# Loading batch 3's K and Q right behind batch 2's V, with its crossbar transposes placed three slots sooner

## Chip, cores and metric

One core of one Trainium2 chip. The metric is the device time of one execution in microseconds (us).

An execution's time is about 1.7 us longer than the span of its profile (315.07 against 313.4, for instance). Times are compared with times, and spans with spans.

## The reference

Attention over a sliding causal window of 64 tokens, then a low-rank token mixer and a channel MLP. B = 8 batches, H = 8 heads, S = 576 tokens, D = 64, model width 512, hidden width 2048.

```python
scores = q @ k.T / sqrt(D); masked to 0 <= i - j < 64; attn = softmax(scores); x = attn @ v
h  = x.transpose(0, 2, 1) @ U @ V          # over tokens, rank 32
u  = x + h.transpose(0, 2, 1)
out = u + relu(u @ w_ch1) @ w_ch2
```

## The kernel before

The MLP runs over 9 chunks of 512 tokens. Between its groups of matmuls ("slots") the attention of the next batch is woven in. K and Q of the batches from 2 on are loaded by POOL's software DMA queue as float32, cast to bfloat16 on the way, and transposed by SP's DMA transposes (the crossbar). The parts that matter here, with cuts marked:

```python
def load_kq(b, split):              # b >= 2: 5 tiles of K and of Q, ten DMAs on POOL's queue
    ...
    nc.gpsimd.dma_start(out=dst[0:rows, t, :, :],
                        in_=src[b, :, t * P : t * P + rows, :].rearrange("h p d -> p h d"))

def load_v(b): ...                  # five DMAs of 128 KB on POOL's queue (4 into vA, 1 into vB)

def TX(t):                          # tile t: K, then Q, from SP
    def f():
        for dst, src in ((kx, kb), (qx, qb)):
            nc.sync.dma_start_transpose(
                out=dst[:, t, :, :], in_=src[:, t, :, :].rearrange("p h d -> p (h d)"))
    return f
...
CROSS = {                           # chunk: {batch: slots of its five TX}
    0: {2: [16, 17, 18, 19, 20]},
    1: {3: [13, 14, 15, 16, 17], 4: [26, 27, 28, 29, 30]},
    2: {5: [24, 25, 26, 27, 28]},
}
...
def loads(b, *tiles):
    for t in tiles:                 # the "hold": POOL copies one element of a transposed tile,
        nc.gpsimd.tensor_copy(      # so what follows on POOL waits until that transpose landed
            out=held[:], in_=qfs[(b + 1) % 2][0:1, t * HP * P : t * HP * P + 1])
        if t == tiles[0] and len(tiles) > 1:
            load_v(b + 1)
    for _ in load_kq(b + 2, False):
        pass

if 1 < b and b + 1 < B:
    load_v(b + 1)
...
if b == 1:
    slots[20].append(lambda: loads(1, 2, NT - 1))   # hold tile 2, V(2), hold tile 4, K/Q(3)
if b == 2:
    slots[15].append(lambda: loads(2, 2))           # hold tile 2 of batch 3, then K/Q(4)
```

So POOL does, from 60 us on: hold on batch 2's third transpose pair, V(2), hold on batch 2's last transpose, K/Q(3), V(3), hold on batch 3's third transpose pair, K/Q(4). "V(2)" means the V loads of batch 2.

The softmax here doesn't subtract the row's maximum and nothing guards it: scores larger than these inputs give would overflow.

Of the kernel before, what the change touches and what calls it, by code (L numbers as in the profile page):

```python
# [16 lines left out]
def kernel(  # L17
# [63 lines left out]
    NT = 5  # L81
# [28 lines left out]
    def load_kq(b, split):  # L110
        kb, qb = staged(b)
        if b < NGR:
            for h0, h1 in ((0, 4), (4, 8)) if split else ((0, H),):
                hs = slice(h0, h1)
                for t, src in ((kb, k), (qb, q)):
                    nc.gpsimd.dma_start(  # L116
                        out=t[:, hs, :, :].rearrange("p h c d -> p h (c d)"),
                        in_=src[b, hs, :, :].rearrange("h (p c) d -> p h (c d)", c=GR),
                    )
                    yield  # L120
        else:
            for t in range(NT):
                rows = P if t < NFULL else W
                for dst, src in ((kb, k), (qb, q)):
                    nc.gpsimd.dma_start(  # L125
                        out=dst[0:rows, t, :, :],
                        in_=src[b, :, t * P : t * P + rows, :].rearrange("h p d -> p h d"),
                    )
                yield

    def load_v(b):
        for t in range(NFULL + 1):
            dst, lo = (vA[b % 2][:, t], t * P) if t < NFULL else (vB[b % 2][:, NFULL - 1], S - P)
            nc.gpsimd.dma_start(  # L134
                out=dst[:, :, 0:D], in_=v[b, :, lo : lo + P, :].rearrange("h p d -> p h d")
            )

    def shift_v(b, copy):
        va, vb = vA[b % 2], vB[b % 2]
        n = NFULL - 1  # L140
        copy(out=vb[W:P, 0:n, :, :], in_=va[W:P, 0:n, :, :])
        copy(out=vb[0:W, 0:n, :, :], in_=va[0:W, 1 : n + 1, :, :])

    def shift_high(b, copy, t):
        copy(out=vB[b % 2][W:P, t, :, :], in_=vA[b % 2][W:P, t, :, :])

    def shift_low(b, copy, t):
        copy(out=vB[b % 2][0:W, t, :, :], in_=vA[b % 2][0:W, t + 1, :, :])
# [501 lines left out]
    def mlp(c):  # L650
# [93 lines left out]
    PLACE_3 = {**PLACE, "SV": [5, 5, 6, 6]}  # L744
    CROSS = {
        0: {2: [16, 17, 18, 19, 20]},
        1: {3: [13, 14, 15, 16, 17], 4: [26, 27, 28, 29, 30]},
        2: {5: [24, 25, 26, 27, 28]},
    }
    CROSS_N = [20, 21, 22, 23, 24]  # L750
# [77 lines left out]
    for c in range(NCH):  # L828
        slots = all_slots[c]

        def place(b, parts, where):
            if b not in att:
                att[b] = attention(b)
            for part in parts:
                for f, s in zip(att[b][part], where[part]):
                    all_slots[c + s // 100][s % 100].append(f)

        b = c + 1
        if b < B:
            if b == 1:  # L840
                for _ in load_kq(2, False):
                    pass

            def loads(b, *tiles):
                for t in tiles:
                    nc.gpsimd.tensor_copy(  # L846
                        out=held[:],
                        in_=qfs[(b + 1) % 2][0:1, t * HP * P : t * HP * P + 1],
                    )
                    if t == tiles[0] and len(tiles) > 1:  # L850
                        load_v(b + 1)
                for _ in load_kq(b + 2, False):
                    pass

            if 1 < b and b + 1 < B:
                load_v(b + 1)
            if 2 < b and b + 2 < B:
                loads(b, 2)
            where = {1: PLACE_1, 2: PLACE_2, 3: PLACE_3}.get(b, PLACE)
            if b < NXB:  # L860
                place(b, ("T",), where)
            if b == 1:
                place(0, ("V",), PLACE_0)
                slots[6].append(lambda: nc.scalar.copy(out=ub[1][:], in_=uf[1][:]))
            if 3 < b + 1 < B:
                slots[24].append(lambda bs=b + 1: shift_v(bs, nc.vector.tensor_copy))
            if b <= 3:

                def land(t, b=b):
                    def f():  # L870
                        if t < NFULL - 1:
                            shift_high(b, nc.scalar.copy, t)
                        if t > 0:
                            shift_low(b, nc.vector.tensor_copy, t - 1)
                    return f

                att[b]["SV"] = [land(t) for t in range(NFULL)]
                place(b, ("SV",), where)
            place(b, ("S", "M", "PV"), where)
            for n, at in CROSS.get(c, {c + 3: CROSS_N}).items():  # L880
                if n < B:
                    place(n, ("T",), {"T": at})
            place(b, ("U", "V", "UT"), where)
            if b == 1:
                slots[20].append(lambda: loads(1, 2, NT - 1))
            if b == 2:
                slots[15].append(lambda: loads(2, 2))
        for fill, extra in zip(mlp(c) + [lambda: None], slots):
            fill()
            for f in extra:  # L890
                f()
# [30 lines left out]
```

## Time and profile before

| | before |
|---|---|
| median of 3 runs | 313.64 us (313.63 to 318.27) |
| the profiled run | 315.07 us, span 313.4 us |
| PE busy | 306.1 us, 98% |
| PE's wait for batch 3's last transpose | 1.0 us |

The page of the kernel before: engines' busy time and share of the span, then the DMA queues with packets, MB and packet time as a share of the time of 16 engines, then the busy share of the DMA engines in 40 equal slices of the span, in tenths (9 is 90% or more).

```profile
span 313.4 us, 6904 instructions
PE 306.1 (98%) x2875; PEld 150.9 (48%) x2875; DVE 162.2 (52%) x298; ACT 108.6 (35%) x174; POOL 101.3 (32%) x133
q0 software_dynamic: 104720, 18.88, 82.5%
q1 hardware_dynamic: 51744, 20.55, 39.2%
DMA  7999999999999999999999999965100520020012
```

PE is the limit. The DMA engines are busy as well: 90% or more in slices 2 to 26, that is up to about 204 us. (The queues' shares add up packet times that can overlap. They pass 100% in some stretches, so they say nothing of how near a queue is to its limit.) The waits of PE between 50 and 135 us (in total, times, longest), and the chain of waits of the kernel before in that place (start, duration, what):

```profile
PE low L340 <- DMA qf<-qr: 1.0, 1, 1.0
```

```profile
89.14 0.38 SPq L299
...
89.60 5.37 DMA qf<-qr
94.98 0.14 issue
95.11 0.19 PE low L340
```

This is the wait that the change is after. Batch 3's last transpose is issued at 89.60 and lands at 94.98; PE has stood since about 94.0. Behind it stands what POOL and SP do. POOL's timeline of the kernel before (start, duration, engine, line, what; the bracket is idle time and its releaser):

```profile
60.79 0.18 POOL L846 COPY held<-qf 1x1 bf16<-1x1 bf16 x1 [9.38 <-DMA qf<-qr]
61.29 3.53 POOL L134 DMA_DIRECT2D vA<-in_v_dram  x4 [0.32 <-issue]
64.78 0.91 POOL L134 DMA_DIRECT2D vB<-in_v_dram  x1
68.55 0.18 POOL L846 COPY held<-qf 1x1 bf16<-1x1 bf16 x1 [2.85 <-DMA qf<-qr]
69.06 0.89 POOL L125 DMA_DIRECT2D kr<-in_k_dram  x1 [0.34 <-PE psA L663]
...
76.68 0.76 POOL L125 DMA_DIRECT2D qr<-in_q_dram  x1
77.36 3.60 POOL L134 DMA_DIRECT2D vA<-in_v_dram  x4
```

SP's timeline of the kernel before: the first, the seventh and the tenth of batch 3's transposes (SPq is SP's instruction queue).

```profile
74.62 1.20 SPq L299 DMA_TRANSPOSE kf<-kr  x1
...
83.39 3.16 SPq L299 DMA_TRANSPOSE kf<-kr  x1
...
89.60 1.37 SPq L299 DMA_TRANSPOSE qf<-qr  x1
```

### The profile page before, as it was taken

The page shows a single profiled execution, that of the slowest core. Times are in us where ns is not written, and L with a number is a line of the kernel's source. Part 1 is how long each engine was busy: PE and PEld are TensorE (multiplying, and loading weights), DVE is VectorE, ACT ScalarE, POOL GpSimd, SP SyncE. Part 2 cuts the span into 40 slices and gives each one's busy share as a digit, 9 for nine tenths or more (in the row PEclk, how much of TensorE's full clock was granted, in tenths as well). Part 3 has the DMA queues.
Part 4 walks back from the last instruction along what each step waited for, and adds up shares of the span by engine and source line. Part 5 has one row for each costly group of instructions (what it writes and reads, how often), then busy time and mean ns, then how long its engine had stood idle before and what let it go on. Part 6 is the DMA issues. An engine that isn't in the chain of part 4 may idle for free.

```text
span 313.4 us, 6904 instructions
## 1 busy us (share of the span) xinstructions
PE 306.1 (98%) x2875; PEld 150.9 (48%) x2875; DVE 162.2 (52%) x298; ACT 108.6 (35%) x174; POOL 101.3 (32%) x133
## 2 busy tenths in 40 slices
PE   8899999999998999999999999999999999999996
PEld 7554554544444544454445444544454444444443
DVE  4475468337756843684358445744574443016011
ACT  3655660467027520533043404440345003301500
POOL 8683263159439346426543571000000000000000
PEclk9999999999999999999999999999999999999999
DMA  7999999999999999999999999965100520020012
GB/s 104 164 208 208 206 168 146 129 180 192 121 153 200 159 152 147 193 140 159 175 174 156 170 156 158 178 99 131 67 2 2 134 84 2 14 86 33 2 61 73
DMA packets 156495, 39.87 MB, mean 127 GB/s; under 512 B 145040, under 2 KB 151440, under 8 KB 156464
## 3 DMA queue, kind: packets, MB, share of 16 engines
q0 software_dynamic: 104720, 18.88, 82.5%
q1 hardware_dynamic: 51744, 20.55, 39.2%
q8 instruction: 22, 0.36, 0.4%
q14 instruction: 9, 0.07, 0.1%
HBM read 37.97 MB, written 9.44 MB: 151 GB/s over the span
## 4 chain that ended last, share of the span: by engine, by line
PE 81%; DMA 13%; POOL 3%; DVE 2%; issue 1%; SPq 0%; POOLq 0%
PE psU L687 36%; PE psA L663 36%; DMA qr<-in_q_dram 4%; DMA vB<-in_v_dram 4%; DMA vA<-in_v_dram 3%; PE psv L581 2%; PE xw L402 2%; PE sc L340 2%; DMA qf<-qr 2%; DVE xs L469 1%; POOL vA L134 1%; PE pshh L501 1%; POOL kr L116 1%; PE tpu L613 0%; POOL vrep L220 0%
## 5 line engine op out<-in xcount | busy, mean ns | idle before, releaser
L687 PE MATMUL psU<-w2b,c 128*128 128x512 bf16 (+2 forms) x592 | 131.3, 373 | 0.1
L663 PE MATMUL psA<-uTc,w1b 128*128 128x512 bf16 x576 | 131.0, 379 | 0.0
L687 PEld LDWEIGHTS <-c 128*128 128x128 bf16 x592 | 56.6, 98 | 64.8 <-issue 0.5
L663 PEld LDWEIGHTS <-w1b 128*128 128x128 bf16 x576 | 54.2, 98 | 64.4 <-issue 1.8
L675 ACT ACTIVATE c<-psA 128x512 bf16<-128x512 f32 x84 | 50.1, 597 | 88.8 <-PE psA L663 88.2
L697 DVE TENSOR_TENSOR osb<-psU,un 128x512 f32<-128x512 f32 (+2 forms) x37 | 24.9, 677 | 76.7 <-PE psU L687 76.3
L673 DVE TENSOR_SCALAR c<-psA 128x512 bf16<-128x512 f32 x60 | 41.3, 689 | 25.5 <-PE psA L663 25.5
L594 DVE TENSOR_TENSOR un<-psv,xs 128x512 bf16<-128x512 f32 (+1 forms) x40 | 25.5, 685 | 22.9 <-PE psv L581 22.7
L134 POOL DMA_DIRECT2D vA<-in_v_dram x32 | 28.6, 909 | 17.3 <-PE psU L687 3.1
L360 ACT ACTIVATE pts<-sc 128x1024 bf16<-128x1024 f32 x32 | 31.3, 1028 | 2.7 <-PE sc L340 2.7
L125 POOL DMA_DIRECT2D kr<-in_k_dram x30 | 25.8, 860 | 10.1 <-DMA vA<-in_v_dram 3.5
L125 POOL DMA_DIRECT2D qr<-in_q_dram x30 | 25.9, 864 | 8.9 <-DMA w2b<-in_moe_w_ch_dram 3.2
L393 ACT ACTIVATE ptl<-low 128x256 bf16<-128x256 f32 x6 | 2.3, 384 | 64.4 <-PE high L340 64.4
L366 DVE TENSOR_TENSOR pts<-pts,maskA 128x1024 bf16<-128x1024 bf16 x28 | 19.1, 682 | 1.1 <-ACT pts L360 1.1
L469 DVE TENSOR_TENSOR xs<-xw,rcw 128x896 bf16<-128x896 f32 x14 | 15.3, 1092 | 0.5
L340 PEld LDWEIGHTS <-kf 64*64 64x64 bf16 x704 | 9.9, 107 | 8.8 <-issue 8.2
L846 POOL COPY held<-qf 1x1 bf16<-1x1 bf16 x6 | 1.1, 178 | 39.4 <-DMA qf<-qr 39.4
L581 PE MATMUL psv<-hh,vrep 128*128 128x512 bf16 x40 | 12.5, 379 | 0.0
L402 PEld LDWEIGHTS <-pts 128*64 128x64 bf16 x512 | 10.0, 110 | 4.7 <-issue 3.7
L340 PE MATMUL sc<-qf,kf 64*64 64x128 bf16 (+1 forms) x608 | 11.6, 212 | 0.6 <-DVE qf L293 0.6
L134 POOL DMA_DIRECT2D vB<-in_v_dram x8 | 7.2, 901 | 5.9 <-DMA qr<-in_q_dram 2.5
L616 ACT COPY uTc<-tpu 128x512 bf16<-128x512 bf16 x9 | 5.3, 586 | 10.8 <-PE tpu L613 10.8
(108 smaller groups left out, 171.2 us busy)
## 6 DMA issues: line engine op xcount, KB each, us to landing
out_dram<-osb SPq DMA_DIRECT2D x35, 256.0 KB, 5.0
vA<-in_v_dram POOLq DMA_DIRECT2D x32, 128.0 KB, 13.1
kr<-in_k_dram POOLq DMA_DIRECT2D x24, 128.0 KB, 8.7
qr<-in_q_dram POOLq DMA_DIRECT2D x24, 128.0 KB, 8.9
w2b<-in_moe_w_ch_dram POOLq DMA_DIRECT2D x4, 512.0 KB, 15.7
vB<-in_v_dram POOLq DMA_DIRECT2D x8, 128.0 KB, 13.7
w1b<-in_moe_w_ch_dram POOLq DMA_DIRECT2D x2, 512.0 KB, 10.9
w1b<-in_moe_w_ch_dram POOLq DMA_DIRECT2D x1, 1024.0 KB, 10.0
```

The costliest lines, as they stand in the source:

```text
L125: nc.gpsimd.dma_start(out=dst[0:rows, t, :, :], in_=src[b, :, t * P : t * P + rows, :].rearrange("h p d -> p h d"),)
L134: nc.gpsimd.dma_start(out=dst[:, :, 0:D], in_=v[b, :, lo : lo + P, :].rearrange("h p d -> p h d"))
L340: nc.tensor.matmul(sc[g][r0 : r0 + W, col * W : (col + n) * W], keys_of(j, u, rs), queries_of(j, blk, n, rs), start=not spare, stop=last o ...
L360: nc.scalar.activation(out=dst, in_=sc[:], func=ACT.Exp, scale=scale)
L366: nc.vector.tensor_tensor(out=dst, in0=dst, in1=maskA.rearrange("p g n w -> p g (n w)"), op=ALU.mult)
L581: nc.tensor.matmul(ps[0][:, n, :], vrep[:, off : off + P], hh["sb"][:], start=True, stop=True)
L594: nc.vector.tensor_tensor(out=u_tiles[g][rs, :], in0=ps[0][rs, n, :], in1=x[rs, t, :, :].rearrange("p h d -> p (h d)"), op=ALU.add,)
L663: nc.tensor.matmul(ps[i][:], w1b[:, dc, i * P : (i + 1) * P], uTc[:, :, dc, :], start=(dc == 0), stop=(dc == NDC - 1),)
L673: nc.vector.tensor_relu(out=c1[i][:], in_=ps[i][:])
L675: nc.scalar.activation(out=c1[i][:], in_=ps[i][:], func=ACT.Relu)
L687: nc.tensor.matmul(acc[t][:, lo:hi], c1[i][:, t * P : (t + 1) * P], w2b[:, i, lo:hi], start=(i == 0), stop=(i == NFC - 1),)
L697: nc.vector.tensor_tensor(out=osb[:, lo:hi], in0=acc[t][:, lo:hi], in1=u_tiles[g][:, lo:hi], op=ALU.add,)
```

## The change

The intent: the second hold keeps POOL idle until 68.55 us. Without it, K/Q(3) goes out right behind V(2), batch 3's transposes can start sooner, and PE need not wait at 95 us.

```diff
-        1: {3: [13, 14, 15, 16, 17], 4: [26, 27, 28, 29, 30]},
+        1: {3: [10, 11, 12, 13, 14], 4: [26, 27, 28, 29, 30]},
...
-                    if t == tiles[0] and len(tiles) > 1:
-                        load_v(b + 1)
+                if b == 1:
+                    load_v(b + 1)
                 for _ in load_kq(b + 2, False):
                     pass
...
-                slots[20].append(lambda: loads(1, 2, NT - 1))
+                slots[20].append(lambda: loads(1, 2))
```

## The prediction

> **What bounds the kernel now.** The page gives PE 306.1 us busy of a 313.4 us span, at granted clock 1.0. The waits by engine give PE 3.7 us in all; the only one the change can touch is 1.0 us on "low" (line 340) for DMA qf<-qr. In the chain of waits it ends at 94.98 us: batch 3's last crossbar transpose was issued at 89.60 and landed 5.4 us later. The table of stretches agrees: 94 to 96 us has PE busy 1.00 of 2.00. After 95 us PE never waits for a load, so the ceiling of the gain is about 1.0 us, 0.3%.
>
> **What the change does.** The instruction order of PE, DVE, ACT and SP is the same before and after. So "three slots sooner" moves nothing on SP: the ten transposes follow the same four output stores and start when K's first tile lands. The real edit is one POOL copy less ("held", 0.18 us), whose wait for batch 2's last transpose ended at 68.55. Without it POOL issues batch 3's K/Q from about 65.7 (V's fifth issue: 64.78 plus 0.91) instead of 69.06: 3.4 us sooner.
>
> **How much arrives.** Little of that. Batch 2's V loads, issued 61.3 to 65.7, landed at 66.1, 67.8, 70.0, 71.0 and 73.3, slowed by transposes and four 256 KB stores; K's first tile landed at 74.5. Both are on the software queue, and the Trainium skill (DMA: Bandwidth & Descriptors, "Two DMAs through the same engine are not ordered") says descriptors of one queue on one engine start in order. So K queues behind V: estimate, V's last landing 73.3 plus one tile at the observed pace (0.87 us) = 74.1, 0.4 us sooner. The packets dip for roughly 0.7 us between V's last and K's first, an upper estimate. The transposes follow at SP's pace (74.62 to 89.60, mostly 1.2 to 1.5 us each, one of 3.16 in a DMA stall near 83 us), so their end moves by the same 0.4 to 0.7. Batch 3's V loads come sooner too, so the contention moves along. PE's wait at 95 us should shrink from 1.0 to 0.3-0.6 us.
>
> **Cost.** Batch 2's transposes landed just before 68.5 and PE needs them at 68.81: almost no slack. K/Q descriptors queued from about 67.5 us may slow them where an engine has finished its share of V: 0 to 0.5 us of new PE wait. That also makes PE later at 95, so the two don't add fully.
>
> **Predicted.** 313.2 us, range 312.4 to 314.4. One of three runs before took 318.27, which the range leaves out.
>
> **What would show it.** POOL's timeline: K/Q issues from near 65.7, one held fewer, and a wait at about the eighth issue (eight loads outstanding). First batch 3 transpose on SP between 73.8 and 74.4, not 71. PE's wait at 95 us under 0.7 us, later work shifted by that alone. If the first transpose starts near 71.5, queueing behind V was wrong and the whole 1.0 us is gained. If PE waits on "low" near 69 us, the removed hold had protected batch 2's transposes.
>
> **What would make it wrong.** The stall near 83 us (packets over 1 us long) costs batch 3's transposes about 2 us and is tied to nothing I can see: without it the wait at 95 would be zero already; a longer one costs more. Batch 2's transposes delayed by over 1 us would make the change slightly slower. Nothing comes near 2%.

## The result

Ratios are the mean time of one kernel's runs over that of the other's of the same rounds, so not quite the ratio of the medians. Executions over 1.5% slower than the fastest of the same kernel are left out of the means.

| | before | after |
|---|---|---|
| median | 313.70 us (6 runs, 313.23 to 318.27) | 314.61 us (6 runs, 314.06 to 315.48) |
| ratio to before | 1 | 1.0029 (95%: 1.0007 to 1.0052) |
| span of the profiled run | 313.4 us | 313.4 us |

The time is within 2% of before, as forecast, but on the wrong side: 0.3% longer instead of 0.15% shorter, and 0.2 us above the range. The profiled run of before was one of its long ones, so the two traces have the same span: the difference of the medians can't be read from these two traces alone.

The changed kernel's waits of PE, which answer to the one wait of before:

```profile
PE low L340 <- DMA qf<-qr: 1.0, 1, 1.0
PE xw L402 <- DVE vB L148: 0.3, 1, 0.3
PE psU L687 <- issue: 0.2, 1, 0.2
```

The wait at 95 us has not shrunk, and a second one stands at 104 us. (The third has no releaser that the profile shows.) POOL's timeline after the change:

```profile
60.43 0.18 POOL L846 COPY held<-qf 1x1 bf16<-1x1 bf16 x1 [9.51 <-DMA qf<-qr]
60.94 3.52 POOL L134 DMA_DIRECT2D vA<-in_v_dram  x4 [0.32 <-PE psA L663]
64.41 0.91 POOL L134 DMA_DIRECT2D vB<-in_v_dram  x1
65.28 0.93 POOL L125 DMA_DIRECT2D kr<-in_k_dram  x1
...
70.68 0.88 POOL L125 DMA_DIRECT2D qr<-in_q_dram  x1 [0.97 <-PE psA L663]
...
74.61 0.69 POOL L125 DMA_DIRECT2D qr<-in_q_dram  x1
76.43 3.51 POOL L134 DMA_DIRECT2D vA<-in_v_dram  x4 [1.14 <-DVE vB L148]
```

The hold is gone. K/Q(3) starts at 65.28 instead of 69.06, but its ten issues now have gaps (with eight loads outstanding POOL waits for V(2), whose last three tiles landed at 70.15, 71.07 and 72.53). They end at 74.61, 2 us sooner than before, and V(3) starts 0.9 us sooner. SP's timeline and the chain of waits after the change:

```profile
73.38 1.83 SPq L299 DMA_TRANSPOSE kf<-kr  x1
...
88.98 1.97 SPq L299 DMA_TRANSPOSE qf<-qr  x1
```

```profile
88.98 5.75 DMA qf<-qr
94.73 0.14 issue
94.86 0.19 PE low L340
...
103.45 0.59 DVE vB L148
...
104.08 0.39 PE xw L402 x13
```

The wait at 104 us is not one for a load: V(3) had landed by 93.79. DVE worked without a pause from 99.93 us on, and PE waited for its copy into vB.

The first transpose went out 1.24 us sooner, and the last one landed only 0.25 us sooner. Since this run's V(2) also started 0.35 us sooner (60.94 against 61.29), the last landing is, counted from there, not sooner at all: 33.8 us after V(2)'s first issue against 33.7. Below, this count "from V(2)'s first issue" is used for all traces, because it takes out how fast PE and the weights' loads got through the first 60 us. The landings come from the trace's times from issue to landing.

### The profile page after: what moved, and what is told of

Same layout as the page of the kernel before. It is cut to its first block, busy times and chain, and to the rows that moved or that the text cites. A ratio compares the mean times of both kernels' runs of the same rounds, so it can differ in the third digit from the quotient of the medians.

```text
span 313.4 us, 6881 instructions
## 1 busy us (share of the span) xinstructions
PE 304.5 (97%) x2852; PEld 151.0 (48%) x2875; DVE 162.5 (52%) x298; ACT 108.6 (35%) x174; POOL 100.8 (32%) x132
## 4 chain that ended last, share of the span: by engine, by line
PE 92%; DVE 4%; DMA 2%; ACT 1%; issue 1%; SPq 0%
PE psA L663 39%; PE psU L687 37%; PE sc L340 3%; PE psv L581 3%; PE xw L402 2%; DMA qf<-qr 2%; PE unread L757 2%; PE tpg L276 1%; DVE xs L469 1%; PE pshh L501 1%; ACT pts L360 1%; DVE c L673 1%; PE xr L402 1%; PE tpm L276 0%; DVE qf L293 0%
## 5 line engine op out<-in xcount | busy, mean ns | idle before, releaser
L687 PE MATMUL psU<-w2b,c 128*128 128x512 bf16 (+2 forms) x573 | 130.0, 374 | 1.2 <-issue 0.2
```

The lines of the kernel that those rows point to most:

```text
L687: nc.tensor.matmul(acc[t][:, lo:hi], c1[i][:, t * P : (t + 1) * P], w2b[:, i, lo:hi], start=(i == 0), stop=(i == NFC - 1),)
```

## The experiments

All kernels here compute the right result. Each came with six runs (e5: five) and one trace. "Baseline" is the kernel before as run between the others in the same rounds. After "Measured" stand the ratio to the baseline, its 95% interval and the median.

### e1 and e2: controls

e1 is the kernel before, unchanged. e2 is the slots alone:

```diff
-        1: {3: [13, 14, 15, 16, 17], 4: [26, 27, 28, 29, 30]},
+        1: {3: [10, 11, 12, 13, 14], 4: [26, 27, 28, 29, 30]},
```

> The kernel before, unchanged, as a control (A/A) and to see a second profile of it. Theory P (typical run of before has no wait at 95 us): the profiled run of before took 315.07 us with span 313.4, while its other runs have a median of 313.7, about 1.4 us less; so this kernel's typical span should be near 312.0, and its profile should show the PE wait on low for DMA qf<-qr at 95 us as under 0.3 us instead of 1.0. Rival N (noise only): ratio to before 1.000 within 0.001, but the wait at 95 us stays about 1.0 us also in this profile.

> Only the slots of batch 3's transposes moved (10 to 14), the hold kept. The instruction order of every engine is that of before, waits too. Theory: the same time as before, ratio 1.000 within 0.0015. Rival: if the slots matter by something that the instruction order does not show, the ratio is that of the whole change, 1.003.

Measured: e1 0.9991 (0.9969 to 1.0013), 314.02 us, PE's wait at 95 us 0.5 us. e2 1.0002 (0.9980 to 1.0025), 314.61 us, no wait at 95 us. Theory P was half right: e1's trace has a shorter wait, but not under 0.3 us, and its span is 312.7 us, not 312.0. The slots do nothing, which the unchanged instruction order of SP said. The same program has the wait with 1.0, 0.5 or 0 us: it is not a fixed cost. In e2 PE came later (it had waited 1.0 us for Q loads in the first 50 us), and by then the transposes were there.

### e3 and e4: the hold alone, and the whole change again

e3 takes the change without the slots; e4 is the change.

> Only the second hold removed, the slots of batch 3's transposes left at 13 to 17. Theory: all of the change's effect is here, ratio 1.002 to 1.004 to before, equal to the whole change within 0.001, and POOL's K/Q issues from about 65.5 us. Rival (slots carry it): ratio 1.000.

> The whole change once more, on the same chip as the three others. Theory: ratio 1.002 to 1.004 (0.6 to 1.2 us), PE wait at 95 us of about 1 us in its profile as before, and a wait of about 0.3 us on DVE's copy into vB at 104 us. Rival N (chip to chip noise): ratio within 0.001 of 1.000.

Measured: e3 1.0027 (0.9996 to 1.0057), 315.41 us; e4 1.0020 (0.9995 to 1.0046), 314.85 us. Both in the expected range, neither interval clear of 1. e3's trace has no wait at 95 us (PE was late), e4's has 1.0 us; neither had 0.3 us at 104 us, so that expectation failed.

### e5 and e6: the place in the row, and the missing instruction

e5 is the change as the first of its row. e6 is the change, with the second hold put back on tile 2, which the first hold has waited for already, so that it holds nothing. Against the kernel before, with the slots and the line that keeps V(2) between the two copies cut:

```diff
...
-                slots[20].append(lambda: loads(1, 2, NT - 1))
+                slots[20].append(lambda: loads(1, 2, 2))
```

> The whole change a third time, now first in the row of kernels instead of last, to rule out that its place in the row made it slow. Theory C (the loss is real: batch 3's transposes end no sooner though they start about 1 us sooner, because V(3), issued sooner too, shares the DMA engines with them until it drains): ratio to before 1.002 to 1.003, and the last transpose of batch 3 lands 33.2 to 33.8 us after V(2)'s first issue, as in the three traces without the hold (33.8, 33.2, 33.8); those with the hold gave 33.7, 33.4, 32.7. Rival O (order of the runs, or noise): ratio within 0.001 of 1.000.

> The change with the second POOL copy put back, but reading tile 2's transpose, which the first copy has already waited for, so that it holds nothing: as many POOL instructions as before, K/Q as early as after the change. Theory C (what matters is when the loads come): as the change, ratio 1.002 to 1.003. Rival I (an instruction less, so another placement of the program): as before, ratio 1.000.

Measured: e5 1.0010 (0.9986 to 1.0035), 314.49 us; e6 1.0030 (0.9998 to 1.0063), 315.10 us. e5 fell on the border between the theories. e6 leans against the missing instruction as the cause, though its interval doesn't exclude 1. Last landing after V(2)'s first issue: 33.8 in e5, 34.8 in e6. e6's profiled run was its slowest (317.3 us), and shows what a longer wait does. PE's waits of e6, then the table of stretches from 95 to 100 us of e6 and, after it, of the kernel before (length; busy time and count of PE, PEld, DVE, ACT, POOL; granted clock; DMA share; GB/s):

```profile
PE low L340 <- DMA qf<-qr: 2.1, 1, 2.1
```

```profile
95.00:100.00 5.00, 4.08 (x60) 1.86 (x61) 1.71 (x3) 2.49 (x4) 5.00 (x7) 0.66 2.04 216
```

```profile
95.00:100.00 5.00, 4.89 (x105) 2.71 (x106) 2.91 (x5) 3.87 (x6) 5.00 (x8) 1.00 2.24 185
```

After a wait of 2.1 us the granted clock was 0.66 in these 5 us (0.50 from 96.58 on, for 3.41 us); after one of 1.0 us it stayed at 1.00. The stretch from ACT's first exponential of batch 3 to its copy of the low-rank product took 16.9 us instead of the 15.2 of the traces without any wait in it. So this wait of 2.1 us cost about 1.7 us more. The Trainium skill ("TensorE: Matmul & The Clock Gate", "Part 1: The HAM clock gate") puts the drop after an idle window of about 3.4 us; here a shorter wait sufficed. Where the limit lies is not shown: in e12 (below) the clock fell to 0.50 at 14.40 us though PE's longest wait in the 10 us before was 1.1 us, while e3's wait of 1.6 us near 13 us left it at 1.00.

### e7 and e8: V(3) late

V(3) is put behind the hold on batch 3's third transpose pair; e7 with the change, e8 with the hold kept. e7 against the changed kernel:

```diff
-            if 1 < b and b + 1 < B:
+            if 2 < b and b + 1 < B:
                 load_v(b + 1)
...
-                if b == 1:
+                if b <= 2:
                     load_v(b + 1)
```

> The change, and batch 3's V loads put behind the POOL copy that waits for batch 3's second pair of transposes after the first (tile 2), so they start near 81 us instead of 76. Theory C: the transposes have the DMA engines to themselves until then, the last one lands near 90 to 92 us instead of 94.5 to 95, PE's wait at 95 us is gone, and the time falls below that of the change by 0.7 to 1.2 us: ratio to before 0.997 to 0.999. Rival S (the end of the transposes is set by their start and SP's issue pace, not by V): the last transpose still lands after 94 us and the ratio is that of the change. Risk: V(3) late for the copies into vB near 100 us.

> The kernel before, and batch 3's V loads put late in the same way. Theory C: the last transpose lands near 91 to 93 us, no PE wait at 95 us, ratio to before 0.997 to 0.999, the same as the late V without the hold within 0.001: with V out of the way the hold is worth nothing. If the one without the hold stays 0.002 or more slower than this one, the hold costs somewhere else than at 95 us.

Measured: e7 1.0029 (1.0003 to 1.0055), 314.91 us; e8 1.0026 (1.0000 to 1.0051), 314.81 us. The half of theory C that concerns the DMA engines held: with V(3) started at 86.7 and 86.3 us (later than I had expected, as the third pair lands late), the last transpose landed at 92.4 and 91.9 instead of 94 to 95, and PE's wait at 95 us was gone in both. The half that concerns the time failed. PE's waits from 50 to 135 us, e7 and then e8:

```profile
PE psA L663 <- DMA uTc<-un: 1.4, 1, 1.4
```

```profile
PE xw L402 <- DVE vB L148: 0.5, 1, 0.5
PE psA L663 <- DMA uTc<-un: 0.4, 1, 0.4
```

About a microsecond came back at the next places where PE waits for others: for DVE's copies into vB near 104 us, and for the crossbar transposes of u near 126 us. Only the second is a wait for a DMA. In e8 V(3) had landed by 96.33 us, and DVE worked without a pause from 98.71 until the copy was done. Over all traces the copies in this place took 0.27 to 0.81 us, and each one over 0.3 us overlapped a load issue of POOL (others that did so took 0.28; why was not tried). e7 and e8 agree within 0.0003, as theory C had it.

### e9 and e12: V(3) in the middle

A third hold, on the first transpose pair of batch 3, ahead of V(3); e9 with the old hold kept, e12 with the change. The same `if 2 < b` as in e7, and:

```diff
+                def mid_v():
+                    nc.gpsimd.tensor_copy(out=held[:], in_=qfs[1][0:1, 0:1])
+                    load_v(3)
+
+                slots[14].append(mid_v)
                 slots[15].append(lambda: loads(2, 2))
```

> The kernel before, with batch 3's V loads held only until batch 3's first transpose pair (tile 0) has landed, so from about 82.5 us instead of 76.7 (before) or 86.3 (late V). Theory C (V(3) and batch 3's transposes share the DMA engines, what one gains the other pays): the last transpose lands at about 92.5 to 94 us and PE's wait at 95 us falls under 0.3 us, K/Q(4) start no later than before, so nothing is paid at 127 us; ratio 0.997 to 0.9995. Rival D (DMA work is the limit in the whole stretch, and each delay is paid later): the loss only moves to 104 us (DVE's copies into vB) or 127 us, ratio 1.000 to 1.003.

> The change, with batch 3's V loads held until batch 3's first transpose pair has landed. Theory C: as the same edit with the hold within 0.001, PE's wait at 95 us under 0.3 us, ratio to before 0.997 to 1.000. If it is slower by 0.002 than the one with the hold, taking the hold away costs something that V(3) has no part in.

Measured: e9 1.0020 (0.9996 to 1.0043), 314.75 us; e12 1.0014 (0.9990 to 1.0038), 314.81 us. Neither beats before. The traces show no wait at 95 us, but that is no proof: in both PE had lost about 1 us waiting for Q loads in the first 50 us and came late (in e12 the clock had fallen as well, to 0.50 for 3.4 us from 14.40 us), and the last landings (94.2 and 94.4 us) are hardly sooner than before. The traces show a likely reason: K/Q(4) went out at 88.1 and 87.8 us instead of 91.6, across the last transposes, whose final one needed 7.0 and 7.1 us to land. So K/Q(4) took the place of V(3) beside them. Rival D fits these times better; where the untraced runs lose is not seen.

### e10: the transposes later, the loads early

The change, with batch 3's transposes in another order, so that the first must wait for a later K tile:

```diff
-            pcs["T"] = [TX(t) for t in range(NT)]
+            pcs["T"] = [TX(t) for t in ((1, 0, 2, 3, 4) if b == 3 else range(NT))]
```

> The change, but batch 3's transposes go in the order tile 1, 0, 2, 3, 4, so the first waits for the second K tile: they start about 1 to 2 us later (first issue on SP about 75.5 to 76.5 instead of 73.4 to 74.9), with the loads as early as after the change. Theory C: their start does not set their end; the last one still lands 33.0 to 33.9 us after V(2)'s first issue, and the ratio to before is that of the change within 0.001. Rival S (the prediction's step: the end moves with the start): the last one lands 1 to 2 us later, PE's wait at 95 us is 2 to 3 us, and the ratio 1.005 to 1.009.

SP's timeline of e10, the first and the last of the ten; then the time from issue to landing of the last one; then PE's wait:

```profile
76.20 1.20 SPq L299 DMA_TRANSPOSE kf<-kr  x1
...
90.37 1.22 SPq L299 DMA_TRANSPOSE qf<-qr  x1
```

```profile
qf<-qr SPq DMA_TRANSPOSE x1, 2.5
```

```profile
PE psA L663 <- DMA uTc<-un: 0.9, 1, 0.9
```

Started 2.8 us later than in the change's own trace (76.20 against 73.38), the transposes ended 1.9 us sooner: the last was issued at 90.37 and landed 2.5 us later, at 92.84 us, 31.9 us after V(2)'s first issue. Rival S is refuted in that trace. My own expectation (33.0 to 33.9) was off too, on the other side. V(3) also ended sooner, at 90.4 us instead of 93.8. So the engines did the same work in less time. A shorter stall near 83 us (see below) is not the reason: SP's longest issue, which marks it, took 2.5 us here and 2.4 in e18, against 2.1 to 3.4 in the 13 traces of the first two rows of the table below.

But the kernel was slower: 1.0048 (1.0018 to 1.0078), 315.83 us. The traced run, one of the shorter (314.82 us), lost 0.9 us at 126 us; where the longer ones lost is not seen. It was not to a fallen clock: the granted clock of all six was 0.998 or more.

### e11, and e13 to e16: is the loss real?

> The kernel before again, as a control and for one more trace with the hold. Theory C: ratio 1.000 within 0.0015, PE's wait at 95 us 0 to 1 us, the last transpose of batch 3 lands 32.6 to 33.7 us after V(2)'s first issue (without the hold 33.2 to 34.8).

e11: 1.0019 (0.9984 to 1.0054), 314.75 us, wait of 0.9 us at 95 us, last landing at 33.6. A copy of before came out as slow as the change, so the place in the row matters about as much as the effect sought. Hence two of each in alternation:

> First of four in alternation (after, before, after, before) on one chip. Theory C (real loss, small): the two copies of the change have a mean of fast runs 0.4 to 0.9 us above that of the two copies of the kernel before. Rival O (place in the row and noise): less than 0.2 us apart. In the trace the last transpose of batch 3 lands 33.2 to 34.0 us after V(2)'s first issue.

> Second of four. Theory C: 0.4 to 0.9 us below the two copies of the change. Rival O: equal to them. In the trace the last transpose of batch 3 lands 32.6 to 33.7 us after V(2)'s first issue, in spite of a first transpose issued about 0.5 to 1 us later than in the change.

> Third of four, as the first: theory C ratio to before 1.001 to 1.003, rival O 1.000 within 0.0007.

> Fourth of four, as the second: theory C ratio to before 0.999 to 1.001, rival O equal to the two copies of the change within 0.2 us.

Measured ratios: 1.0012, 0.9999, 1.0018, 1.0014, in that order (each about plus or minus 0.0026). The two copies of the change have a mean of 314.87 us, those of before 314.57: 0.3 us apart, with a standard error of about 0.3. That is between what theory C and rival O expected. Put together: 35 runs without the hold (e3 to e6, e13, e15) have a mean of 315.00, 30 with it (e1, e2, e11, e14, e16) 314.52, standard errors 0.14 each. That is a loss of about 0.5 us, 0.15%, only just clear of the noise. With exact copies alone (23 runs of e4, e5, e13, e15 against 24 of e1, e11, e14, e16) it is 0.3 us with a standard error of 0.2. So the change does not gain; that it loses is likely and not certain.

The 35 and the 30 runs come from several rows and chips. The copies of the kernel before also stand 0.2 us above the 55 baseline runs of the five rows (314.30), so a ratio of an experiment to its baseline whose interval only just excludes 1, like e7's, is not clear of that. What the traces show is clearer than the times. Microseconds after V(2)'s first issue, batch 3's transposes:

| hold | traces | first issued, mean (range) | last landed, mean (range) |
|---|---|---|---|
| kept | before, e1, e2, e11, e14, e16 | 13.5 (13.3 to 14.0) | 33.3 (32.7 to 33.7) |
| removed | after, e3 to e6, e13, e15 | 12.9 (12.0 to 13.5) | 33.7 (33.2 to 34.8) |
| removed, transposes later | e10 | 15.2 | 31.9 |
| kept, transposes later | e18 (below) | 14.4 | 32.3 |

### e17 and e18: later still, and later with the hold

e17 is e10 with the order 2, 0, 1, 3, 4; e18 is the order of e10 with the hold kept.

> The change with batch 3's transposes in the order tile 2, 0, 1, 3, 4: the first waits for the third K tile, first issue about 77 us, 16 to 17 us after V(2)'s first issue. Theory M (mixing wastes DMA time): the last transpose lands 31.5 to 33.0 us after V(2)'s first issue, sooner than in the change (33.2 to 34.8) although it started 3 us later, and no PE wait at 95 us; PE, earlier at 126 us, waits there for the transposes of u up to 1 us. Rival S (start plus SP's pace sets the end): it lands 36 us or more after V(2)'s first issue, PE waits 2 us or more at 95 us.

> The kernel before (hold kept) with batch 3's transposes in the order tile 1, 0, 2, 3, 4: first issue about 76.5 us, 15 to 16 us after V(2)'s first issue. Theory M: the last one lands 31.5 to 33.0 us after V(2)'s first issue (before: 32.7 to 33.7), no or under 0.3 us of PE wait at 95 us; the time within 0.3% of before, since PE then meets the transposes of u at 126 us. Rival S: it lands 1.5 us later than before, 34.5 or more, PE waits 1.5 us or more at 95 us, ratio 1.003 or more with the loss in that place.

e18: 1.0016 (0.9994 to 1.0037), 314.68 us. First issue at 14.4, last landing at 32.3 us after V(2)'s first issue, no wait at 95 us: as theory M had it, and e10's finding seen a second time. Part of the microsecond again came back, this time at 104 us:

```profile
PE xw L402 <- DVE vB L148: 0.6, 1, 0.6
```

e17: 1.0185 (1.0154 to 1.0215), 320.59 us; the last landing at 37.2. The expectation failed, and for a reason I had built in: the hold ahead of K/Q(4) waits for tile 2, which now was the first to be transposed. POOL's timeline and PE's wait of e17:

```profile
87.20 0.18 POOL L846 COPY held<-qf 1x1 bf16<-1x1 bf16 x1 [6.76 <-DMA qf<-qr]
```

```profile
PE low L340 <- DMA qf<-qr: 4.2, 1, 4.2
```

K/Q(4) went out at 87.7 instead of 91.6, across the last transposes, whose final one, issued at 90.97, needed 7.0 us to land instead of e10's 2.5. PE waited 4.2 us, and the granted clock was 0.74 and 0.57 in the two stretches of 5 us after 95 us. So e17 does not tell the theories apart as planned, but it shows once more what loads beside transposes do.

## Why the prediction was wrong

**The step that failed** is "The transposes follow at SP's pace [...], so their end moves by the same 0.4 to 0.7". The start did move as forecast: 0.7 us sooner on average over the traces, first issue at 73.4 to 74.9 us (in the change's own trace 73.38, a little sooner than the 73.8 to 74.4 named). The end did not follow: instead of 0.4 to 0.7 us sooner it lies 0.4 us later on average (33.7 against 33.3, with a standard error of 0.3: "not sooner" is shown, "later" is not). The prediction took the transposes for a chain that its start and SP's pace set. It did see that V(3) would come sooner too, but wrote that "the contention moves along", and gave it no cost. The transposes share the 16 DMA engines with the rest of K/Q(3) and with V(3) nearly all the way, and what sets the end is mostly when all of that is done. e7 and e8 show that V(3) takes part in setting the end: with V(3) out of the way the last transpose landed at 31.6 and 31.1 us after V(2)'s first issue. The packets of the kernel before show the sharing: the DMA queues in stretches of 2 us, for 59 to 61 (transposes alone), 74 to 76 (loads alone) and 88 to 90 us (both):

```profile
q1 hardware_dynamic: 1598, 0.38, 96.9%
```

```profile
q0 software_dynamic: 2450, 0.31, 242.6%
```

```profile
q0 software_dynamic: 923, 0.12, 88.9%
q1 hardware_dynamic: 795, 0.19, 75.8%
```

Side by side, each runs at 923/2450 = 0.38 and 795/1598 = 0.50 of what it does alone, 0.87 together; with the 2051 transpose packets that 58 to 60 us of the changed kernel's trace held, 0.77. So an eighth to a quarter of the engines' rate is lost while both run (an estimate from these counts of single stretches; alone, both may be held by their issue, so the loss may be larger). If so, starting the transposes sooner puts more of them beside the loads and lengthens both. Starting them later, in e10 and e18, let transposes and V(3) both end sooner (in e18 the landing of V(3)'s fifth tile is not recorded; the fourth came at 90.48 us, against 92.44 in the kernel before). That mixing wastes the engines' time fits all these traces and was foreseen for e18. It was not measured by itself, so it is the best explanation and not a proven one. The Trainium skill ("DMA: Bandwidth & Descriptors", "Issuing engines are not separate DMA queues") says that DMAs of all issuing engines run on the same 16 engines and interleave. The trace agrees; I had cited that page for the order within one queue and not drawn this consequence.

**The queueing of K behind V was right.** In the changed kernel K's first tile landed at 73.24, just after V(2)'s last at 72.53, though issued 3.8 us sooner than before. In all seven traces without the hold it landed after V(2)'s last. Also right: the slots do nothing (e2), POOL waits with eight loads outstanding, and no new wait near 69 us.

**"After 95 us PE never waits for a load" was read from one trace, and leaves out what a sooner PE would meet.** Where the wait at 95 us was gone because the transposes landed sooner, PE met the next ones: 0.6 us at 104 us (e18), 0.5 at 104 and 0.4 at 126 us (e8), 0.9 and 1.4 us at 126 us (e10, e7). e11, a copy of the kernel before, waited 0.3 us at 104 after 0.9 at 95, and e15, a copy of the change, 0.6 us at 126 after 0.6 at 95. So even the full 1.0 us would hardly have been won. Where the wait at 95 us was short or gone because PE came late (e1, e2, e16), no new one over 0.2 us followed; PE had then waited 3.1 to 3.9 us in the first 50 us, against 2.7 in the trace of before. Up to 126 us PE must meet others' work at three places close to each other (the DMA engines at 95 and 126 us, DVE at 104), and what it gains at one it can lose at the next.

**The wait of 1.0 us was not typical.** It is 0 to 1.0 us in the six traces with the hold, depending on how late PE comes. The profiled run took 315.07 us where the median was 313.64.

**The centre was too low as well.** I took 313.64, the median of three runs, as the level. In other rows copies of the kernel before average 314.5 and its baselines 314.3. Of the 1.4 us between 313.2 and 314.61, about 0.45 is the gain that did not come, 0.3 to 0.5 the loss, and the rest the level and noise. A range of 2 us was too narrow for a kernel whose own runs spread over 2 to 3 us.

**The stall near 83 us** was called tied to nothing. It has a companion in every trace. The DMA queues of the kernel before from 82 to 84 us hold one packet of another kind:

```profile
q0 software_dynamic: 1130, 0.14, 361.1%
q1 hardware_dynamic: 424, 0.10, 58.9%
q8 instruction: 1, 0.02, 3.7%
```

In each of the 20 traces (both kernels' and e1 to e18's) an instruction packet of 16 KB stands within about 1 us of the longest of SP's ten issues (before: packet at 82.86, issue at 83.39 with 3.16 us). That they go together is seen; that the packet causes the stall was not tried.

**Open:** whether and how much the change loses (0.5 or 0.3 us, each with a standard error of 0.2; PE's waits from 50 to 135 us average 1.1 us in the seven traces without the hold and 0.7 in the six with it, a difference no clearer than that of the times), and where the untraced runs of e9, e10 and e12 lose.

## What to carry to other kernels

Where two DMA streams share the engines and the later one is awaited, ask when all of the shared work ends, not when its first piece can start: here a transposing stream that started later beside loads ended sooner, and the loads too (e10, e18). A wait in one profile is worth its length only if no other deadline follows closely; look for the next places where the waiting engine needs others' work, and take several traces, since the wait may belong to that run alone. For effects under half a per cent, run unchanged copies of the kernel in the same row: here a copy alone came out up to 0.19% off its own baseline.

## What the Trainium skill lacked or had wrong

- "DMA: Bandwidth & Descriptors" says that DMAs of different issuers interleave on the same engines, but gives no cost for DMA transposes beside ordinary loads. Here loads and transposes ran at 0.38 and 0.50 of their own rates side by side (single stretches of one trace), and a transpose that landed 2.4 us after its issue alone took 5 to 9 us beside loads, the wait behind earlier transposes included.
- "Runtime: NRT & Kernel Launch", "Instruction fetch mechanics", says that instructions are fetched in blocks of 16 KiB by DMA and calls the cost mostly hidden. In all 20 traces such a packet stands beside SP's longest transpose issue, 1.6 to 3.4 us where 1.2 to 1.5 are usual (cause not tried).
- "TensorE: Matmul & The Clock Gate", "Part 1: The HAM clock gate", has the clock fall after an idle window of about 3.4 us. Here a PE wait of 2.1 us was followed by a granted clock of 0.50 for 3.41 us (e6; PE was busy for 1.3 of the 3.41 us before the fall). In e12 the clock fell in the same way at 14.40 us after a wait of 1.1 us, with PE busy for 2.0 of the 3.41 us before. Waits of 1.0 us at 95 us, and one of 1.6 us in e3, left it at 1.00. So the length of one wait does not decide it.
